# An FFT with a feed-forward layer on one core: fewer float32 units, an earlier split of w_out, one low half on VectorE, a longer hand-written order

## The chip, the cores and the metric

The kernel runs on one core of a Trainium2 chip. The metric is the device time of one execution in microseconds, lower is better. Engines are named as the profile does: PE (TensorE matmul), PEld (its weight loads), DVE (VectorE), ACT (ScalarE), POOL (GpSimd), SP (SyncE, whose queue issues most DMAs). L432 is line 432 of the kernel before.

## The reference

```python
# x: (8, 3008, 256) float32;  w_in: (256, 2048), w_out: (2048, 256), both float64
X = np.fft.fft(np.fft.fft(x, axis=1), axis=2).real.astype(np.float32)
X = X.reshape(8 * 3008, 256)
h = X @ w_in
g = np.where(h >= 1, h, np.where(h <= -1, 0.0, (h + 1) ** 2 / 4))
return (g @ w_out).astype(np.float32)
```

## The kernel before

**Mathematics.** The 3008 points of the sequence are taken as 47 x 64. Stage 1 multiplies by a 47-point transform (`stage1_sums`, the tiles `y` into a PSUM bank, copied to `z`), stage 2 by a 64-point one (`stage2_sums`, `z` into a bank, split into `pqh` and `pql` by `stage2_split`). The transform over the 256 channels is multiplied into w_in once, on the chip (`fold_w_in`, `fold_low`: the tiles `wh`, `wl`). Position s and its mirror image -s come out of the same two products: u - v and u + v.

**Number format.** float32 operands are split in a high part (`fp32r`, one pass of PE) and a low part, the remainder. A product is then three matmuls: high by high, low by high, high by low. "Native" units instead do one true float32 matmul in the second product, which the profile shows as two records. The weights come as float64 and are taken apart on the chip as integers: `convert_fields` (DVE), `convert_floats` (ACT, three instructions), `convert_join` and `convert_scale` (DVE), for 16 pieces of 128x512 (`jobs`): pieces 0, 1, 4, 5, 8, 9, 12, 13 are of w_in, the others of w_out. `split_w_out(q)` makes `woh` (ACT) and `wol` (DVE) from an eighth of w_out.

**Units.** A unit i is one batch b, one chunk k of columns (482, 512 or 512 wide) and one tile f of 128 of the 2048 inner features. There are 384. In batch 0, units 0 to 23 are features 0 to 7 for the three chunks, units 24 to 47 features 8 to 15. Each unit has
- `gemm1(i)`: 6 matmuls into two `uv` banks (of three in all); DVE makes `us` (L376) and the two halves of `h` (L378, L379); ACT makes `a` in two instructions (L382, L383);
- `activate(i)`: DVE takes min and max (L391 or L394). For units that aren't native, ACT copies the high part `gh` (L397) and POOL subtracts to get the low part `gl`, in two instructions of half a tile each (L399);
- `gemm2(i)`: the second product into four `acc` banks, issued in turn i + 4 (`LAG`).

**Order.** The main loop takes turns i = 0 to 387. A turn traces: `gemm1(i)`, then `activate(i - 1)` (or i, from `PINNED` on), then the letters of `STEPS[i]`, then pieces of the next batch's transform, then `gemm2(i - 4)`. Up to turn `PINNED` - 1 `pin()` chains each engine's instructions in just this order. Later instructions are placed by the compiler's scheduler, which may also put them into earlier gaps. The letters of `START` and `STEPS` are single steps: l load of a raw piece, x load of input, a b c v the four conversions, o `split_w_out`, f and s the two halves of the w_in fold, e `spread_delta` (PE writes a bank with tag `fft`, ACT copies it), p stage sums, z and w `stage1_copy` (w puts half on DVE), q `stage2_split`, y `fold_x`.

**Buffers.** Tiles of one tag share a few slots: `h` and `a` have three each, and the conversions of even pieces use `h`, those of odd pieces `a`. `fft` is one PSUM bank. The raw pieces of w_out and the later ones of w_in lie in the tiles `woh` and `wol` until the split needs these.

Of the kernel before, what the change touches and what calls it, by code (L numbers as in the profile page):

```python
# [37 lines left out]
def _constants():  # L38
# [26 lines left out]

START = (
# [3 lines left out]
)  # L70
STEPS = {
    0: "c4 v4 a5 b5",
    1: "c5 v5 a2 b2",
    2: "f2 f3 c2 v2 a3 b3 s2 s3",
    3: "e1 c3 v3 a6 b6",
    4: "c6 v6 p11 q11",
    5: "a7 b7",
    6: "c7 v7 p12 q12",
    7: "a8 b8",
    8: "c8 v8",  # L80
    9: "a9 b9",
    10: "c9 v9 a10 b10",
    11: "f4 f5 s4 s5",
    12: "e2 c10 v10 p13 q13",
    13: "a11 b11",
    14: "c11 v11 p14 q14",
    15: "o0 o1 a12 b12",
    16: "c12 v12 o2",
    17: "o3 a13 b13",
    18: "c13 v13 o4",  # L90
    19: "o5 a14 b14",
    20: "f6 f7 s6 s7",
    21: "e3 c14 v14 a15 b15",
    22: "o6 c15 v15",
    23: "o7",
}

RAW = {0: "gh", 1: "gh", 4: "gh", 5: "gh", 2: "woh", 3: "woh", 6: "woh", 7: "woh"}
RAW |= {8: "wol", 9: "wol", 10: "wol", 11: "wol", 12: "xt", 13: "xt", 14: "xt", 15: "xt"}

EARLY_BANKS = 13
NATIVE = NFT
PINNED = 18
NEXT = 18


# [1 line left out]
def fft_ffn_kernel(ctx: ExitStack, tc: tile.TileContext, x, cst, w_in, w_out, out):  # L108
    nc = tc.nc

    wts = ctx.enter_context(tc.tile_pool(name="wts", bufs=1))
    sb = ctx.enter_context(tc.tile_pool(name="sb", bufs=1))
    dr = ctx.enter_context(tc.tile_pool(name="dr", bufs=1, space=bass.MemoryType.DRAM))
    ps = ctx.enter_context(tc.tile_pool(name="ps", bufs=1, space=bass.MemoryType.PSUM))

    xt, yt, zt, nyb, pq = {}, {}, {}, {}, {}

    def load_x(b, q):
        tag = "xt" if b or q < 4 else "gl"
# [31 lines left out]
    def fft_bank(b, name):  # L151

        if b == 0 and early[0] < EARLY_BANKS:
            early[0] += 1
            return ps.tile([P, CH], F32, tag=f"acc{early[0] % 4}", name=name, bufs=1)
        return ps.tile([P, CH], F32, tag="fft", name=name, bufs=1)
# [6 lines left out]
    jobs = []  # L163
    for f4 in range(4):
        jobs += [("in", f4, 0), ("in", f4, 1), ("out", 2 * f4), ("out", 2 * f4 + 1)]
    raws, f32s, wo32, shared = {}, {}, {}, {}

    def load_w(n):
        kind, *at = jobs[n]
        if RAW[n] in ("woh", "wol"):  # L170
            if RAW[n] not in shared:
                shared[RAW[n]] = sb.tile([P, 4, CH, 2], U32, tag=RAW[n], name=f"raw_{RAW[n]}", bufs=1), iter(range(4))
            t, slots = shared[RAW[n]]
            raw = t[:, next(slots)]
        else:
            raw = sb.tile([P, CH, 2], U32, tag=RAW[n], name=f"raw_{n}", bufs=4)
        if kind == "in":
            src = w_in.bitcast(U32).rearrange("(h p) (o x) -> h p o x", p=P, x=2 * CH)[at[1], :, at[0] : at[0] + 1]
        else:
            m = CH // D * P  # L180
            src = w_out[at[0] * m : (at[0] + 1) * m, :].bitcast(U32).rearrange("(f p) x -> p f x", p=P)
        nc.sync.dma_start(raw.rearrange("p e two -> p (e two)").rearrange("p (f x) -> p f x", f=src.shape[1]), src)
        raws[n] = raw
# [24 lines left out]
    def convert_scale(n, eng):  # L208
        t, _ = cv.pop(n)
        kind, q, *_ = jobs[n]  # L210
        man, exp = (t[:, i].bitcast(F32) for i in range(2))
        dst = man
        if kind == "in":
            f32s[n] = man
        else:
            if q % 2 == 0 and q < 6:
                pair = sb.tile([P, 2, CH], F32, tag="gl", name=f"wo_{q // 2}", bufs=4)
                wo32[q], wo32[q + 1] = pair[:, 0], pair[:, 1]
            elif q >= 6:
                wo32[q] = man  # L220
            dst = wo32[q]
        eng.tensor_tensor(dst, man, exp, op=ALU.mult)
# [42 lines left out]
    s1, s2 = {}, {}  # L265
# [14 lines left out]
    def stage1_last(b, bank):  # L280
        pd = bank[:NA, GPC * 96 : GPC * 96 + 2 * NC]
        for m in range(2):
            nc.scalar.activation(zt[b][m * NA : (m + 1) * NA, :, P], pd[:, m * NC : (m + 1) * NC], AF.Copy)

    def stage1_copy(b, q, vector=False):
        z, bank = zt[b], s1.pop((b, q))
        if q == 0 and b:
            stage1_last(b, bank)
        pt = bank[:, : GPC * 96].rearrange("p (i n) -> p i n", i=GPC)
        for h in range(2):  # L290
            for m in range(2):
                src = pt[h * NA : (h + 1) * NA].rearrange("p i (t m c) -> p m c (i t)", t=2, m=2)[:, m]
                dst = z[m * NA : (m + 1) * NA, :, (2 * q + h) * 8 : (2 * q + h + 1) * 8]
                if vector and h:
                    nc.vector.tensor_copy(dst, src)
                else:
                    nc.scalar.activation(dst, src, AF.Copy)  # L297
    def stage1(b, q):
        for p in range(q, min(q + 2, XC)):
            if (b, p) in xt and (b, p) not in yt:  # L300
                fold_x(b, p)
        stage1_sums(b, q)
        stage1_copy(b, q)
# [55 lines left out]
    n_units = len(units)  # L359
    per = NCHUNK * NFT  # L360

    fronts, acts = {}, {}

    def gemm1(i):
        b, k, f = units[i]
# [20 lines left out]
    def activate(i):  # L386
        n = WIDTH[units[i][1]]
        h, a = fronts.pop(i)
        if i < NATIVE:
            g = sb.tile([P, 2, CH], F32, tag="gh", name=f"g_{i}", bufs=4)[:, :, :n]  # L390
            nc.vector.scalar_tensor_tensor(g, a, 1.0, h, op0=ALU.min, op1=ALU.max)  # L391
            acts[i] = (g,)
            return
        nc.vector.scalar_tensor_tensor(h, a, 1.0, h, op0=ALU.min, op1=ALU.max)  # L394
        gh = sb.tile([P, 2, CH], F32R, tag="gh", name=f"gh_{i}", bufs=4)[:, :, :n]
        gl = sb.tile([P, 2, CH], F32R, tag="gl", name=f"gl_{i}", bufs=4)[:, :, :n]
        nc.scalar.activation(gh, h, AF.Copy)  # L397
        for sg in range(2):
            nc.gpsimd.tensor_tensor(gl[:, sg], h[:, sg], gh[:, sg].bitcast(F32), op=ALU.subtract)  # L399
        acts[i] = gh, gl  # L400

    accs, parts, outs = {}, {}, {}

# [5 lines left out]
    def gemm2(i):  # L409
# [8 lines left out]
        for dh in range(2):  # L418
# [4 lines left out]
            for sg in range(2):  # L423
                acc = accs[dh * 2 + sg]
                if i < NATIVE:
                    wo_at = (f % 2) * D + dh * P
# [22 lines left out]
            elif last and i < n_units - 1:  # L449
                nc.sync.dma_start(out[b, k, dh].rearrange("s p t -> p s t")[:, :, :n], o[:, :, :n])  # L450

    warm = sb.tile([P, CH], F32, tag="us", name="warm", bufs=2)
    nc.gpsimd.memset(warm, 0.0)
    warm_bank = fft_bank(0, "warm")
    for _ in range(9):
        nc.tensor.matmul(warm_bank, warm[:, :P], warm, start=True, stop=True)

    n1 = XC

    def piece_sums(n):  # L460
# [25 lines left out]
        "s": fold_low,  # L486
        "o": split_w_out,
        "e": spread_delta,
        "t": lambda n: stage1_last(0, s1[0, 0]),
    }  # L490

    def run_steps(names):
        for s in names.split():
            steps[s[0]](int(s[1:] or 0))
# [16 lines left out]
    for i in range(n_units + LAG):  # L511
        if i < n_units:
            b, r = divmod(i, per)
            r0 = NEXT if b == 0 else 0
            if r == r0:
                pending = fft_pieces(b + 1) if b + 1 < NB else []
                done, total = 0, sum(w for w, _ in pending)
                if pending:
                    for q in range(4):
                        load_x(b + 1, q)  # L520
            gemm1(i)
            if b == 0 and r > per // 2 and r % (NFT // 2) == NFT // 2 - 2:
                load_parts(units[i][1])
            if i <= PINNED and i:
                activate(i - 1)
            if i >= PINNED:
                activate(i)
            run_steps(STEPS.get(i, ""))

            change = r % NFT == LAG  # L530
            while pending and (change or r % NFT != LAG - 1 and done < total * (r + 1 - r0) / (per - r0)):
                change = False
                w, f = pending.pop(0)
                f()
                done += w
                k1 = n1 + 7 - len(pending)
                if 4 <= k1 + 3 < XC:
                    load_x(b + 1, k1 + 3)
        if i >= LAG:
            gemm2(i - LAG)  # L540
        if i < PINNED:
            pin()
# [54 lines left out]
```

## Time and profile before

| | |
|---|---|
| median of 3 runs | 1781.17 us (1780.04 to 3464.34) |
| profiled execution, its own time | 1778.06 us |
| its span, first to last instruction | 1776.3 us |
| PE busy | 1744.0 us (98%), 7858 matmuls |
| DVE busy | 1438.4 us (81%) |
| ACT busy | 1344.3 us (76%) |
| POOL busy | 1164.7 us (66%) |

The page of the profile cuts the span into 40 slices of 44.4 us. The windows view sums each engine's busy time in any stretch that is asked for; the timeline view lists instructions in order of start, with the idle time before each in brackets and what ended it. A row of the timeline begins with start and duration in us. A busy PE is not PE at its peak: instructions overlap, and at half clock the same matmul counts double.

### The profile page before, as it was taken

The page shows a single profiled execution, that of the slowest core. Times are in us where ns is not written, and L with a number is a line of the kernel's source. Part 1 is how long each engine was busy: PE and PEld are TensorE (multiplying, and loading weights), DVE is VectorE, ACT ScalarE, POOL GpSimd, SP SyncE. Part 2 cuts the span into 40 slices and gives each one's busy share as a digit, 9 for nine tenths or more (in the row PEclk, how much of TensorE's full clock was granted, in tenths as well). Part 3 has the DMA queues.
Part 4 walks back from the last instruction along what each step waited for, and adds up shares of the span by engine and source line. Part 5 has one row for each costly group of instructions (what it writes and reads, how often), then busy time and mean ns, then how long its engine had stood idle before and what let it go on. Part 6 is the DMA issues. An engine that isn't in the chain of part 4 may idle for free.

```text
span 1776.3 us, 21601 instructions
## 1 busy us (share of the span) xinstructions
PE 1744.0 (98%) x7858; PEld 1407.5 (79%) x7858; DVE 1438.4 (81%) x1762; ACT 1344.3 (76%) x1575; POOL 1164.7 (66%) x813
## 2 busy tenths in 40 slices
PE   7989999999999999999999999999999999999998
PEld 5556788888888888888888888888888888887876
DVE  6979888788887788878878778877888788888886
ACT  5657876887777777778777877778778787777775
POOL 0005866876677766677667776677666766767776
PEclk8999999999999999999999999999999999999999
DMA  9003222110010110101001110011000000000000
GB/s 287 0 23 104 91 73 72 40 54 19 24 42 27 50 42 1 51 27 53 30 4 57 45 31 25 10 51 50 28 24 33 1 23 31 12 24 8 16 24 24
DMA packets 29962, 72.49 MB, mean 41 GB/s; under 512 B 2976, under 2 KB 8224, under 8 KB 29856
## 3 DMA queue, kind: packets, MB, share of 16 engines
q1 hardware_dynamic: 29820, 71.12, 12.3%
q8 instruction: 61, 1.00, 0.2%
q14 instruction: 45, 0.37, 0.1%
q10 hardware_dynamic: 36, 0.01, 0.0%
HBM read 43.31 MB, written 27.81 MB: 40 GB/s over the span
## 4 chain that ended last, share of the span: by engine, by line
PE 67%; POOL 9%; ACT 8%; DVE 8%; issue 6%; DMA 1%; POOLq 0%; ACTq 0%; SPq 0%; DVEq 0%
PE acc L432 42%; PE uv L373 21%; POOL gl L399 9%; DVE h L394 4%; ACT a L383 3%; ACT gh L397 3%; PE s L336 2%; ACT a L382 2%; PE s L274 2%; DVE h L378 1%; DMA x<-in_x_dram 1%; DVE h L379 1%; POOL y L129 1%; ACT z L297 0%; DVE us L376 0%
## 5 line engine op out<-in xcount | busy, mean ns | idle before, releaser
L399 POOL TENSOR_TENSOR gl<-h,gh 128x512 fp32r<-128x512 f32 (+1 forms) x736 | 1057.7, 1460 | 448.2 <-ACT gh L397 408.1
L394 DVE SCALAR_TENSOR_TENSOR h<-a,h 128x1024 f32<-128x1024 f32 (+1 forms) x368 | 555.0, 1508 | 220.3 <-ACT a L383 218.7
L397 ACT ACTIVATE gh<-h 128x1024 fp32r<-128x1024 f32 (+1 forms) x368 | 384.1, 1044 | 343.1 <-DVE h L394 330.5
L432 PE MATMUL acc<-gh,woh 128*128 128x512 f32 (+1 forms) x1472 | 585.9, 398 | 2.7 <-DVE o L443 1.6
L432 PE MATMUL acc<-gl,woh 128*128 128x512 f32 (+1 forms) x1472 | 574.5, 390 | 0.9 <-POOL gl L399 0.9
L432 PE MATMUL acc<-gh,wol 128*128 128x512 f32 (+1 forms) x1472 | 574.2, 390 | 0.0
L382 ACT ACTIVATE a<-h,biases 128x1024 f32<-128x1024 f32 (+1 forms) x384 | 431.7, 1124 | 38.4 <-DVE h L379 36.3
L383 ACT ACTIVATE a<-a 128x1024 f32<-128x1024 f32 (+1 forms) x384 | 398.9, 1039 | 7.5
L432 PEld LDWEIGHTS acc<-gh,woh 128*128 128x128 f32 x1472 | 277.3, 188 | 63.3 <-DVE o L443 4.8
L432 PEld LDWEIGHTS acc<-gl,woh 128*128 128x128 f32 x1472 | 277.2, 188 | 62.0 <-POOL gl L399 2.0
L373 PE MATMUL uv<-pqh,wh 128*128 128x512 f32 (+1 forms) x768 | 308.7, 402 | 12.5 <-DVE us L376 5.7
L432 PEld LDWEIGHTS acc<-gh,wol 128*128 128x128 f32 x1472 | 277.0, 188 | 54.4 <-issue 0.2
L378 DVE TENSOR_TENSOR h<-us,uv 128x512 f32<-128x512 f32 (+1 forms) x384 | 259.8, 676 | 66.3 <-POOL gl L399 22.5
L373 PE MATMUL uv<-pql,wh 128*128 128x512 f32 (+1 forms) x768 | 300.6, 391 | 0.0
L373 PE MATMUL uv<-pqh,wl 128*128 128x512 f32 (+1 forms) x768 | 300.4, 391 | 0.0
L376 DVE SCALAR_TENSOR_TENSOR us<-nyb,delta,uv 128x512 f32<-128x512 f32 (+1 forms) x384 | 278.9, 726 | 19.0 <-PE uv L373 18.7
L379 DVE TENSOR_TENSOR h<-us,uv 128x512 f32<-128x512 f32 (+1 forms) x384 | 256.3, 667 | 0.0
L373 PEld LDWEIGHTS uv<-pqh,wh 128*128 128x128 f32 x768 | 144.5, 188 | 57.9 <-DVE us L376 10.0
L373 PEld LDWEIGHTS uv<-pqh,wl 128*128 128x128 f32 x768 | 144.8, 189 | 32.0 <-issue 3.6
L373 PEld LDWEIGHTS uv<-pql,wh 128*128 128x128 f32 x768 | 144.7, 188 | 30.1 <-DVE pql L160 0.4
L129 POOL TENSOR_TENSOR y<-x 96x512 f32<-96x512 f32 x56 | 101.8, 1817 | 45.4 <-PE uv L373 37.9
L297 ACT ACTIVATE z<-s 64x192 f32<-64x192 f32 x246 | 83.4, 339 | 7.0 <-PE s L274 2.6
(61 smaller groups left out, 660.9 us busy)
## 6 DMA issues: line engine op xcount, KB each, us to landing
x<-in_x_dram SPq DMA_DIRECT2D x64, 384.0 KB, 3.3
out_dram<-o SPq DMA_DIRECT2D x26, 512.0 KB, 2.8
out_dram<-o SPq DMA_DIRECT2D x14, 482.0 KB, 2.9
nyb<-nyr SPq DMA_DIRECT2D x24, 256.0 KB, 3.2
raw<-in_moe_w_in_dram SPq DMA_DIRECT2D x6, 512.0 KB, 9.2
raw_woh<-in_moe_w_out_dram SPq DMA_DIRECT2D x4, 512.0 KB, 8.3
part<-o SPq DMA_DIRECT2D x4, 512.0 KB, 4.5
os<-part SPq DMA_DIRECT2D x4, 512.0 KB, 3.7
```

The lines of the kernel that those rows point to most:

```text
L129: (engine or nc.gpsimd).tensor_tensor(y, t[:, 0], t[:, 1], op=ALU.add)
L297: nc.scalar.activation(dst, src, AF.Copy)
L373: nc.tensor.matmul(t[:, :n], w[m][:, cols], r[:, m, :n], start=(j == 0), stop=(j == 2))
L376: nc.vector.scalar_tensor_tensor(us, nyb[b, k][:, :n], delta[:, f : f + 1], uv[0], op0=ALU.mult, op1=ALU.add)
L378: nc.vector.tensor_tensor(h[:, 0], us, uv[1], op=ALU.subtract)
L379: nc.vector.tensor_tensor(h[:, 1], us, uv[1], op=ALU.add)
L382: nc.scalar.activation(a, h, AF.Relu, bias=half, scale=0.5)
L383: nc.scalar.activation(a, a, AF.Square)
L394: nc.vector.scalar_tensor_tensor(h, a, 1.0, h, op0=ALU.min, op1=ALU.max)
L397: nc.scalar.activation(gh, h, AF.Copy)
L399: nc.gpsimd.tensor_tensor(gl[:, sg], h[:, sg], gh[:, sg].bitcast(F32), op=ALU.subtract)
L432: nc.tensor.matmul(acc[:, :n], w, g[:, sg], start=(begin and j == 0), stop=(last and j == len(terms) - 1))
```

## The change

- `NATIVE` goes from 16 to 8: units 8 to 15 do the second product in three fp32r matmuls.
- `woh` and `wol` are tiles of their own from the start. The raw pieces lie elsewhere (tags `xt`, `pqh`, `pql`). Pieces 10 to 15 are loaded in turns 7 and 11 instead of at the start. The splits o0 to o7 go from turns 15 to 23 to turns 4, 5, 7, 8, 14, 16, 24 and 26; the conversions of pieces 9 to 15 and the folds f4 to f7 move by one to three turns.
- Up to unit 27 the second half of `gl` is made by DVE, in a closure that turn i + 2 calls ahead of `gemm1(i + 2)`; POOL keeps the first half. From unit 28 on POOL makes both.
- `PINNED` goes from 18 to 28. In pinned turns `gemm2(i - 4)` is traced ahead of the next batch's pieces.
- In `START`, y7 goes ahead of w5, and two and four dummy matmuls of 128 columns (`keep_warm`, letter i) follow on p6 and p7. The dummies write the `fft` bank; `warm` goes to tag `a`.
- The copies of batch 0 into `z` no longer wait for each other.

```diff
-    "a0 b0 a1 b1 c0 v0 y0 p0 t0 z0 c1 y1 v1 p1 p8 z1 n0 l2 l3 l6 l7 n1 l8 l9 l10 l11 n2 l12 l13 l14 l15 "
-    "y2 y3 f0 p2 z2 p3 s0 y4 w3 f1 y5 p4 p5 y6 s1 w4 e0 p6 w5 y7 p7 w6 w7 p9 p10 q9 q10 a4 b4"
+    "a0 b0 a1 b1 c0 v0 y0 p0 t0 z0 c1 y1 v1 p1 p8 z1 n0 l2 l3 l6 l7 n1 l8 l9 n2 "
+    "y2 y3 f0 p2 z2 p3 s0 y4 w3 f1 y5 p4 p5 y6 s1 w4 e0 p6 y7 w5 i2 p7 w6 w7 i4 p9 p10 q9 q10 a4 b4"
 STEPS = {
     0: "c4 v4 a5 b5",
     1: "c5 v5 a2 b2",
     2: "f2 f3 c2 v2 a3 b3 s2 s3",
     3: "e1 c3 v3 a6 b6",
-    4: "c6 v6 p11 q11",
-    5: "a7 b7",
+    4: "c6 v6 o0 p11 q11",
+    5: "a7 b7 o1",
     6: "c7 v7 p12 q12",
-    7: "a8 b8",
-    8: "c8 v8",
-    9: "a9 b9",
-    10: "c9 v9 a10 b10",
-    11: "f4 f5 s4 s5",
-    12: "e2 c10 v10 p13 q13",
-    13: "a11 b11",
-    14: "c11 v11 p14 q14",
-    15: "o0 o1 a12 b12",
-    16: "c12 v12 o2",
-    17: "o3 a13 b13",
-    18: "c13 v13 o4",
-    19: "o5 a14 b14",
-    20: "f6 f7 s6 s7",
-    21: "e3 c14 v14 a15 b15",
-    22: "o6 c15 v15",
-    23: "o7",
+    7: "l10 l11 l12 l13 o2 a8 b8",
+    8: "c8 v8 o3",
+    10: "a9 b9",
+    11: "c9 v9 l14 l15",
+    12: "f4 f5 s4 s5",
+    13: "e2 a10 b10",
+    14: "c10 v10 o4 p13 q13",
+    15: "p14 q14 a11 b11",
+    16: "c11 v11 o5",
+    17: "a12 b12",
+    18: "c12 v12",
+    19: "a13 b13",
+    20: "c13 v13",
+    22: "f6 f7 s6 s7",
+    23: "e3 a14 b14",
+    24: "c14 v14 o6",
+    25: "a15 b15",
+    26: "c15 v15 o7",
 }
-RAW = {0: "gh", 1: "gh", 4: "gh", 5: "gh", 2: "woh", 3: "woh", 6: "woh", 7: "woh"}
-RAW |= {8: "wol", 9: "wol", 10: "wol", 11: "wol", 12: "xt", 13: "xt", 14: "xt", 15: "xt"}
-EARLY_BANKS = 13
-NATIVE = NFT
-PINNED = 18
+RAW = {0: "gh", 1: "gh", 4: "gh", 5: "gh", 2: "xt", 3: "xt", 6: "xt", 7: "xt"}
+RAW |= {8: "pqh", 9: "pql", 10: "xt", 11: "xt", 12: "xt", 13: "xt", 14: "pqh", 15: "pql"}
+EARLY_BANKS = 12
+NATIVE = NFT // 2
+PINNED = 28
...
-                    nc.scalar.activation(dst, src, AF.Copy)
+                    ins = nc.scalar.activation(dst, src, AF.Copy)
+                if b == 0:
+                    if q:
+                        tc.declare_no_dep(ins.ins, group="z", reason="other columns")
+                    tc.add_to_no_dep_group("z", ins.ins)
...
         nc.scalar.activation(gh, h, AF.Copy)
-        for sg in range(2):
-            nc.gpsimd.tensor_tensor(gl[:, sg], h[:, sg], gh[:, sg].bitcast(F32), op=ALU.subtract)
         acts[i] = gh, gl
+        low_half(i, h, 0, nc.gpsimd)
+        if i < PINNED:
+            lows[i] = lambda: low_half(i, h, 1, nc.vector)
+        else:
+            low_half(i, h, 1, nc.gpsimd)
+
+    def low_half(i, h, sg, eng):
+        gh, gl = acts[i]
+        eng.tensor_tensor(gl[:, sg], h[:, sg], gh[:, sg].bitcast(F32), op=ALU.subtract)
...
-    warm = sb.tile([P, CH], F32, tag="us", name="warm", bufs=2)
+    warm = sb.tile([P, CH], F32, tag="a", name="warm", bufs=3)
     nc.gpsimd.memset(warm, 0.0)
-    warm_bank = fft_bank(0, "warm")
-    for _ in range(9):
-        nc.tensor.matmul(warm_bank, warm[:, :P], warm, start=True, stop=True)
+    warm_bank = ps.tile([P, CH], F32, tag="fft", name="warm_bank", bufs=1)
+
+    def keep_warm(n, width=P):
+        for _ in range(n):
+            nc.tensor.matmul(warm_bank[:, :width], warm[:, :P], warm[:, :width], start=True, stop=True)
+
+    keep_warm(9, CH)
...
+            if i - 2 in lows:
+                lows.pop(i - 2)()
             gemm1(i)
...
-            if i <= PINNED and i:
+            if 0 < i <= PINNED:
                 activate(i - 1)
             if i >= PINNED:
                 activate(i)
             run_steps(STEPS.get(i, ""))
-
+        if i >= LAG and i < PINNED:
+            gemm2(i - LAG)
+        if i < n_units:
             change = r % NFT == LAG
...
-        if i >= LAG:
+        if i >= PINNED:
             gemm2(i - LAG)
```

More of the change, by code (lines that the diff above doesn't have):

```diff
@@ L165, in fft_ffn_kernel @@
         jobs += [("in", f4, 0), ("in", f4, 1), ("out", 2 * f4), ("out", 2 * f4 + 1)]
-    raws, f32s, wo32, shared = {}, {}, {}, {}
+    raws, f32s, wo32 = {}, {}, {}
     def load_w(n):
         kind, *at = jobs[n]
[L170 to L176, printed above, removed]
+        raw = sb.tile([P, CH, 2], U32, tag=RAW[n], name=f"raw_{n}", bufs=4)
         if kind == "in":
@@ L215, in convert_scale @@
         else:
-            if q % 2 == 0 and q < 6:
+            if q % 2 == 0 and q < NATIVE // 2:
                 pair = sb.tile([P, 2, CH], F32, tag="gl", name=f"wo_{q // 2}", bufs=4)
                 wo32[q], wo32[q + 1] = pair[:, 0], pair[:, 1]
-            elif q >= 6:
+            elif q >= NATIVE // 2:
                 wo32[q] = man
@@ L294, in stage1_copy @@
                 if vector and h:
-                    nc.vector.tensor_copy(dst, src)
+                    ins = nc.vector.tensor_copy(dst, src)
                 else:
-                    nc.scalar.activation(dst, src, AF.Copy)
+                    ins = nc.scalar.activation(dst, src, AF.Copy)
[3 more added lines that the diff above has]
+                    tc.add_to_no_dep_group("z", ins.ins)
     def stage1(b, q):
@@ L360, in fft_ffn_kernel @@
     per = NCHUNK * NFT
-    fronts, acts = {}, {}
+    fronts, acts, lows = {}, {}, {}
     def gemm1(i):
@@ L488, in fft_ffn_kernel @@
         "e": spread_delta,
+        "i": keep_warm,
         "t": lambda n: stage1_last(0, s1[0, 0]),
```

## Prediction

> **What bounds the kernel now.** I read the page, then the windows by stage, then the timelines of turns 0 to 28. u_i below is the start of `us` of unit i on VectorE: u_4 is 58.11, u_10 is 87.28, u_18 is 140.76 and u_28 is 201.81, and the first three windows are cut there.
>
> ```profile
> span 1776.3 us, 21601 instructions
> PE 1744.0 (98%) x7858; PEld 1407.5 (79%) x7858; DVE 1438.4 (81%) x1762; ACT 1344.3 (76%) x1575; POOL 1164.7 (66%) x813
> ```
>
> ```profile
> core 0: us, PE busy (x) PEld busy (x) DVE busy (x) ACT busy (x) POOL busy (x), PEclk, DMA share, GB/s
> 58.11:87.28 29.17, 29.17 (x95) 17.38 (x95) 26.96 (x42) 19.08 (x23) 0.00 (x0) 0.97 0.00 1
> 87.28:140.76 53.48, 48.72 (x149) 27.22 (x147) 41.28 (x62) 30.63 (x41) 1.88 (x3) 0.94 0.08 26
> 140.76:201.81 61.05, 54.76 (x241) 40.74 (x242) 55.29 (x66) 48.91 (x73) 43.29 (x32) 1.00 0.31 97
> 302.00:1702.00 1400.00, 1397.61 (x6448) 1156.56 (x6447) 1137.57 (x1357) 1085.06 (x1237) 997.73 (x689) 1.00 0.09 30
> ```
>
> From 302 to 1702 TensorE is busy 1397.61 of 1400 us, and the change leaves that code alone. So whatever the change wins or loses before u_28 reaches the end unshortened. Ahead of it TensorE sets the pace only in turns 4 to 9 (29.17 of 29.17); in 10 to 17 it misses 4.8 us, in 18 to 27 6.3 us, and VectorE is busy 26.96 of 29.17 and 55.29 of 61.05: there is hardly room on it for more.
>
> **Part 1, the head: a gain.**
>
> ```profile
> 24.49 0.69 DVE L129 TENSOR_TENSOR y<-x 96x512 f32<-96x512 f32 x1
> 25.32 1.64 PE L274 MATMUL s<-cs,y 96*128 96x96 f32 x8 [1.35 <-DVE y L129]
> 27.71 0.73 DVE L295 COPY z<-s 64x192 f32<-64x192 f32 x2 [1.89 <-ACT z L297]
> 26.00:28.00 2.00, 0.96 (x5) 0.72 (x4) 0.29 (x1) 0.67 (x2) 0.00 (x0) 0.50 1.04 400
> 28.59 3.75 PE L336 MATMUL s<-cs,z 128*128 128x128 f32 x16 [1.63 <-DVE z L295]
> 68.45 1.05 PE L336 MATMUL s<-cs,z 128*128 128x128 f32 x8
> ```
>
> p7 (25.32) waited 1.35 us for y7, which stood behind w5; ahead of it, y7 is done about 0.9 us earlier. The last `z` copies on VectorE (27.71) started when ScalarE's ended; without that tie they run beside them, 0.7 less. The clock was 0.50 and p9, p10 took 3.75 us for 16 records; at full clock 8 records take 1.05, so 2 x 0.9 when the dummies hold the clock (they lie in the waits and cost at most 0.4). p7 itself, 1.64, would be 0.9 like them, 0.7 less. Together 0.9 + 0.7 + 0.7 + 1.9 = **-4.2 us** for u_0; bounds 0 (clock still halved, raw loads in the way) and -4.6. Turns 0 to 3 keep their letters, and the loads that leave the head were waited for by nobody there: nothing.
>
> **Part 2, turns 4 to 9: the splits.**
>
> ```profile
> 63.67 0.71 DVE L376 SCALAR_TENSOR_TENSOR us<-nyb,delta,uv 128x482 f32<-128x482 f32 x1
> 67.03 0.42 DVE L193 TENSOR_SCALAR cv<-raw_woh 128x512 uint32<-128x512 uint32 x1
> 69.05 0.72 ACT L200 ACTIVATE cv<-cv,biases 128x512 uint32<-128x512 f32 x1
> 68.00 0.72 DVE L376 SCALAR_TENSOR_TENSOR us<-nyb,delta,uv 128x482 f32<-128x482 f32 x1 [0.55 <-PE uv L373]
> 73.56 0.71 DVE L376 SCALAR_TENSOR_TENSOR us<-nyb,delta,uv 128x482 f32<-128x482 f32 x1
> 78.03 0.75 DVE L376 SCALAR_TENSOR_TENSOR us<-nyb,delta,uv 128x512 f32<-128x512 f32 x1 [0.68 <-PE uv L373]
> 83.08 0.74 DVE L376 SCALAR_TENSOR_TENSOR us<-nyb,delta,uv 128x512 f32<-128x512 f32 x1
> 124.09 0.63 ACT L159 ACTIVATE woh<-wo 128x512 fp32r<-128x512 f32 x1 [0.36 <-DVE wo L222]
> 125.24 0.68 DVE L160 TENSOR_TENSOR wol<-wo,woh 128x512 fp32r<-128x512 f32 x1
> ```
>
> A split is a 0.63 us copy on ScalarE, then a 0.68 us subtraction on VectorE (0.6 from start to start). In turn 5 ("a7 b7 o1") ScalarE is in b7 until 69.77, 6.1 us after u_5; only then comes woh, ending at 6.7, and VectorE, whose next instruction is wol, stands from 3.8 on with us_6 queued behind it, and TensorE's `uv` banks behind that. u_6 falls 7.3 after u_5 instead of 4.33: +2.9. o0 (turn 4) and o3 (turn 8) follow VectorE work that outlasts the copy: +0.6 each. In turn 7 o2 precedes a8, and woh stands behind `a`: wol starts some 4.8 after `us`, and with 0.6 for it and 0.7 for a8 the turn takes 6.1 instead of 4.47 (73.56 to 78.03), +1.6. Turn 9 is the first of part 3: 6.0 instead of 4.2 (83.08 to 87.28), +1.8. Sum **+7.5**; bounds +2.4 (four subtractions alone) and +9.
>
> **Part 3, the low half on VectorE.** What the change buys is on TensorE:
>
> ```profile
> 114.67 3.43 PE acc L432 x8
> 241.54 2.80 PE acc L432 x12
> 113.27 1.40 PE uv L373 x6
> ```
>
> The chain has a native 512-wide second product at 3.43 us and three fp32r passes at 2.80: 8 x 0.63 = 5.0 us of TensorE, whose turn falls to 1.40 + 2.80 = 4.2. What it adds is a wait, and unit 17 of the kernel before shows every link of it:
>
> ```profile
> 137.58 0.74 DVE L376 SCALAR_TENSOR_TENSOR us<-nyb,delta,uv 128x512 f32<-128x512 f32 x1
> 139.03 0.68 DVE L379 TENSOR_TENSOR h<-us,uv 128x512 f32<-128x512 f32 x1
> 139.74 1.15 ACT L382 ACTIVATE a<-h,biases 128x1024 f32<-128x1024 f32 x1 [2.98 <-DVE h L379]
> 140.92 1.06 ACT L383 ACTIVATE a<-a 128x1024 f32<-128x1024 f32 x1
> 141.89 1.04 ACT L397 ACTIVATE gh<-h 128x1024 fp32r<-128x1024 f32 x1
> 143.00 3.14 POOL L399 TENSOR_TENSOR gl<-h,gh 128x512 fp32r<-128x512 f32 x2 [0.76 <-ACT gh L397]
> 143.48 1.54 DVE L160 TENSOR_TENSOR wol<-wo,woh 128x512 fp32r<-128x512 f32 x1
> 108.57 0.60 ACT L159 ACTIVATE pqh<-s 128x512 fp32r<-128x512 f32 x1 [0.77 <-PE s L336]
> 109.20 0.69 DVE L160 TENSOR_TENSOR pql<-s,pqh 128x512 fp32r<-128x512 f32 x1 [2.07 <-ACT pqh L159]
> ```
>
> In a pinned turn gh(i-1) stands on ScalarE behind both `a` instructions of unit i, which need h_i. It ends at 142.93, 5.35 us after u_17. The low half of unit i-1 needs it, and on VectorE it stands ahead of us_{i+1}. So u_{i+1} is at least 5.35 + 0.03 (VectorE's delay behind ScalarE, 109.17 to 109.20) + 0.60 (the subtraction) = **6.0 us** after u_i, however fast TensorE is; with 482 columns 5.8. Queued behind the waiting half are `us` and both `h` of the next unit, hence ScalarE's next `a` and TensorE's third `uv` bank. This holds from turn 9 to 27. Bounds for a turn: 4.2 (TensorE) and 6.0 + 1.25 (GpSimd first, below); I take 6.0, whose links are all rows.
>
> On top, in turns 10 to 27:
>
> ```profile
> 193.72 0.66 DVE L378 TENSOR_TENSOR h<-us,uv 128x482 f32<-128x482 f32 x1 [1.25 <-POOL gl L399]
> 158.53 1.27 POOL L129 TENSOR_TENSOR y<-x 96x512 f32<-96x512 f32 x1
> 106.45 2.08 PE L336 MATMUL s<-cs,z 128*128 128x128 f32 x8 [4.51 <-ACT delta L241]
> 39.68 0.77 PE L373 MATMUL uv<-pqh,wh 128*128 128x482 f32 x1 [2.31 <-DVE us L376]
> 40.00:42.00 2.00, 2.00 (x4) 1.01 (x4) 2.00 (x4) 1.70 (x2) 0.00 (x0) 0.50 0.99 367
> ```
>
> - Six pairs "copy on ScalarE, subtraction on VectorE" (o4, o5, o6, o7, q13, q14) stand behind gh and ahead of the low half: 6 x 1.2 = 7.2, and 2.2 where GpSimd or a11 falls between: 9.4.
> - Two folds (12, 22): two wh copies, a row and s4, s5 in that place: 2 x 2.9 = 5.8. They cost the same kind before, but beside native units.
> - Turn 11: c9, v9 and two evictions on VectorE, 1.3.
> - Turn 18: the first piece of batch 1 needs two folds of x on GpSimd (1.27 and 0.4) that now stand behind gl(17), 5.4 us into the turn; gemm1(19) is behind the piece on TensorE: +4.7, and 1.3 for a clock that such a wait halves (106.45: 2.08 after 4.51 idle): 6.0.
> - While a conversion or its result holds one of three `h` slots, h_i must wait for GpSimd's half of unit i-2, as at 193.72; 0.55 in eight turns: 4.4.
>
> Fourteen turns at 6.0 and the four of 482 columns at 5.8 make 107.2; with 26.9 on top 134.1, against 53.48 + 61.05 = 114.5 before: **+19.6**. In that the stall of 4.51 at 106.45 is gone already (e2 and p13 now lie in two turns). Bounds: -12 (rival A) to +28 (B).
>
> **The sum.** At u_28 TensorE leads by about one product, of which 2 us are won back: -2. -4.2 + 7.5 + 19.6 - 2 = +20.9 on the profiled execution's 1778.06 us (1.8 above its span): **1799 us**. The median shown, 1781.17, is 3 above that execution, so the forecast is 1.0% over the median. 2% of it, 35.6 us, is about what a measurement of this kernel tells from no change.
>
> **Rivals.**
>
> A, TensorE keeps the pace: 1762. If the low half finds gh ready, turns 4 to 9 stay at 29.2, turns 10 to 27 lose the 5.0 of native work, the stall of 4.51 and some 2.5 of half clock after it, and the head gains 4.2: -16. For it: 98% busy. Against it: row 141.89, which stands behind 140.92 in pinned order. This is the faster side.
>
> B, GpSimd gets there first: 1807. Both halves of gl start on the same gh. At 143.00 GpSimd began 0.07 us after it, and the subtraction at 143.48 lasted 1.54 instead of 0.68. If GpSimd wins in the ten short turns, each is 1.25 longer, less the 4.4 of slot waits: +8. Against it: VectorE reacts to ScalarE in 0.03 us.
> The Trainium skill ("SBUF — State Buffer", section "SBUF: two separate sides") says that the pair of ports is an exclusive lock, held by whichever starts first for its whole instruction. The trace agrees in kind (1.54); no run here shows a DVE and a GpSimd subtraction released at once.
>
> C, the clock falls in every long turn: 1819, slower by over 2%. A turn of 7.3 us or more leaves TensorE 2.5 to 3.4 idle; at 39.68 a wait of 2.31 was followed by clock 0.50. Eight such turns at 2.5 each, nothing hidden, are +20. It decides once gemm1 comes later than VectorE is ready for it. Against it: TensorE runs a product ahead, so most of that is hidden.
> The Trainium skill ("TensorE: Matmul & The Clock Gate", section "HAM oscillation — how this bites in real kernels") wants gaps above about 3.4 us for that. By it only turn 18 would cool and C would cost nothing; row 39.68 speaks against the rule, with one gap.
>
> D, the written order doesn't hold (the scheduler fills the gaps with later units): about 1782.
>
> **How the numbers follow.** Forecast (1788 to 1808) 0.55; A 0.2; B 0.12; C 0.07; D 0.06. The range reaches over B and most of the way to A and C: 1770 to 1815. Faster by over 2% (below 1745.5) 0.02, within 0.92, slower (above 1816.8) 0.06.
>
> **What would show it.** Right: `us` rows 6.0 apart in plain turns 10, 13, 17, 21; a low half on VectorE that starts 0.03 after gh with idle time before it put down to ACT gh; us_6 7.3 after us_5; p9 and p10 at 0.9 each with the first uv near 29; TensorE misses over 30 us between u_10 and u_28. Wrong: `us` rows 4.2 to 5 apart (A), GpSimd's gl ahead of VectorE's low half (B), clock near 0.5 through turns 11 to 18 (C).

## The result, and the profile after

The changed kernel takes 1805.76 us (median of 4 runs, 1803.62 to 1807.05) beside 1780.71 us for the kernel before on the same chip: a ratio of 1.0141, 95% interval [1.0121, 1.0161]. It is 1.4% slower, which is less than the 2% that count as a difference here and more than the measurement's uncertainty. One of the four runs of the kernel before took 3464.34 us and doesn't enter the ratio. The profiled execution took 1803.62 us, 25.6 more than that of before; the forecast was +20.9 and 1799.

In this and the next section a turn's length is the time from one `us` row to the next, and u_i is the start of `us` of unit i (DVE, line 375 of the changed kernel). The page's first lines after:

```profile
span 1801.8 us, 21728 instructions
PE 1751.7 (97%) x7902; PEld 1420.0 (79%) x7902; DVE 1448.0 (80%) x1782; ACT 1351.9 (75%) x1583; POOL 1159.5 (64%) x809
```

PE is busy 7.7 us more although, by the prediction's prices, it was given 5.0 us less to do; in turns 10 to 26 the granted clock, below, is lower than before (0.89 and 0.90 instead of 0.94 and 1.00), and the same matmuls then count longer.

Behind the written order one must count the `us` rows with care. DVE's timeline where it ends, in the changed kernel:

```profile
222.35 1.33 DVE L375 SCALAR_TENSOR_TENSOR us<-nyb,delta,uv 128x482 f32<-128x482 f32 x2
233.59 0.71 DVE L375 SCALAR_TENSOR_TENSOR us<-nyb,delta,uv 128x482 f32<-128x482 f32 x1
```

The first row holds two instructions: the scheduler starts `us` of unit 28 right behind that of unit 27, and 233.59 is u_29. From 222.35 to 233.59 there are thus two turns, 27 and 28. The stages are cut at u_27 for this reason, while the forecast's last stage began at u_28. The windows view of the changed kernel, cut at its own u_4, u_10, u_18 and u_27, then from u_27 and from u_33 to the end; the last two rows are those same tails in the kernel before:

```profile
core 0: us, PE busy (x) PEld busy (x) DVE busy (x) ACT busy (x) POOL busy (x), PEclk, DMA share, GB/s
55.97:92.64 36.67, 34.43 (x107) 19.31 (x106) 29.30 (x45) 22.41 (x28) 0.56 (x1) 0.97 0.21 71
92.64:152.09 59.45, 47.38 (x169) 32.03 (x169) 45.27 (x67) 36.01 (x45) 12.71 (x11) 0.89 0.10 30
152.09:222.35 70.26, 52.46 (x225) 40.36 (x226) 50.33 (x70) 45.65 (x68) 25.84 (x21) 0.90 0.17 55
222.35:1801.80 1579.45, 1571.66 (x7223) 1299.59 (x7222) 1283.52 (x1530) 1213.95 (x1381) 1116.86 (x769) 1.00 0.10 34
249.82:1801.80 1551.98, 1544.46 (x7109) 1276.32 (x7107) 1260.37 (x1502) 1193.31 (x1353) 1098.16 (x757) 1.00 0.10 32
```

```profile
195.93:1776.30 1580.37, 1572.39 (x7239) 1298.05 (x7237) 1279.38 (x1528) 1216.97 (x1387) 1121.69 (x773) 1.00 0.10 34
222.63:1776.30 1553.67, 1545.69 (x7106) 1274.93 (x7104) 1258.50 (x1502) 1193.88 (x1353) 1098.48 (x757) 1.00 0.10 32
```

The first number behind the bounds is the stage's length, the second PE's busy time in it. Beside the kernel before:

| stage | before | after | difference | forecast |
|---|---|---|---|---|
| start to u_0 | 34.35 | 30.86 | -3.5 | -4.2 |
| turns 0 to 3 | 23.76 | 25.11 | +1.35 | 0 |
| turns 4 to 9 | 29.17 | 36.67 | +7.5 | +7.5 |
| turns 10 to 17 | 53.48 | 59.45 | +6.0 | } +19.65 |
| turns 18 to 26 | 55.17 | 70.26 | +15.1 | } |
| behind u_27 | 1580.37 | 1579.45 | -0.9 | -2.1 |

The forecast of +19.6 was for turns 10 to 27; without turn 27 (5.8 by the forecast, 5.88 before) it is 128.3 - 108.65 = +19.65. Measured are +21.1. From u_10 to u_27 PE misses 12.07 + 17.80 = 29.9 us, against 4.8 + 6.3 before. The wait that was forecast is there, link by link. Timelines of DVE and ACT in turn 9 of the changed kernel:

```profile
86.65 0.74 DVE L375 SCALAR_TENSOR_TENSOR us<-nyb,delta,uv 128x512 f32<-128x512 f32 x1
88.82 1.15 ACT L381 ACTIVATE a<-h,biases 128x1024 f32<-128x1024 f32 x1 [2.89 <-DVE h L378]
90.00 1.06 ACT L382 ACTIVATE a<-a 128x1024 f32<-128x1024 f32 x1
90.96 1.04 ACT L396 ACTIVATE gh<-h 128x1024 fp32r<-128x1024 f32 x1
92.03 0.69 DVE L406 TENSOR_TENSOR gl<-h,gh 128x512 fp32r<-128x512 f32 x1 [2.12 <-ACT gh L396]
92.64 0.74 DVE L375 SCALAR_TENSOR_TENSOR us<-nyb,delta,uv 128x512 f32<-128x512 f32 x1
```

`gh` stands behind both `a`; DVE is idle 2.12 us for it, starts the low half 0.03 us after `gh` ends, and `us` can only follow that: 92.64 - 86.65 = 5.99. The forecast was 6.0. Turns 13, 17 and 23 take 6.01, 6.02 and 6.00. Turns 10 and 21, which the prediction named beside 13 and 17, take 6.39 and 6.42: there `h` waits for GpSimd's half as well, 0.50 and 0.53 us. The same view of turn 5, in which the split came behind the conversion:

```profile
67.51 0.72 ACT L195 ACTIVATE cv<-cv,biases 128x512 uint32<-128x512 f32 x1
68.14 0.61 ACT L160 ACTIVATE woh<-wo 128x512 fp32r<-128x512 f32 x1
68.79 0.69 DVE L161 TENSOR_TENSOR wol<-wo,woh 128x512 fp32r<-128x512 f32 x1 [2.87 <-ACT woh L160]
69.39 0.71 DVE L375 SCALAR_TENSOR_TENSOR us<-nyb,delta,uv 128x482 f32<-128x482 f32 x1
```

u_5 was at 62.13, so the turn takes 7.26 (forecast 7.3).

### The profile page after: what moved, and what is told of

Same layout as the page of the kernel before. It is cut to its first block, busy times and chain, and to the rows that moved or that the text cites. A ratio compares the mean times of both kernels' runs of the same rounds, so it can differ in the third digit from the quotient of the medians.

```text
span 1801.8 us, 21728 instructions
## 1 busy us (share of the span) xinstructions
PE 1751.7 (97%) x7902; PEld 1420.0 (79%) x7902; DVE 1448.0 (80%) x1782; ACT 1351.9 (75%) x1583; POOL 1159.5 (64%) x809
## 4 chain that ended last, share of the span: by engine, by line
PE 64%; POOL 8%; ACT 7%; issue 6%; DVE 4%; POOLq 0%; ACTq 0%; DVEq 0%
PE acc L438 40%; PE uv L372 20%; POOL gl L406 7%; DVE h L393 3%; ACT a L382 3%; ACT gh L396 2%; PE s L335 2%; ACT a L381 2%; PE s L269 2%; DVE h L377 0%; POOL y L130 0%; ACT z L292 0%; DVE h L378 0%; DVE o L449 0%; DVE gl L406 0%
## 5 line engine op out<-in xcount | busy, mean ns | idle before, releaser
L393 DVE SCALAR_TENSOR_TENSOR h<-a,h 128x1024 f32<-128x1024 f32 (+1 forms) x376 | 565.0, 1503 | 210.7 <-ACT a L382 209.1
L396 ACT ACTIVATE gh<-h 128x1024 fp32r<-128x1024 f32 (+1 forms) x376 | 392.3, 1043 | 336.1 <-DVE h L393 326.1
L438 PE MATMUL acc<-gh,woh 128*128 128x512 f32 (+1 forms) x1504 | 601.0, 400 | 4.5 <-ACT o L447 1.8
L438 PE MATMUL acc<-gl,woh 128*128 128x512 f32 (+1 forms) x1504 | 587.9, 391 | 0.9 <-POOL gl L406 0.9
L438 PE MATMUL acc<-gh,wol 128*128 128x512 f32 (+1 forms) x1504 | 588.0, 391 | 0.0
L438 PEld LDWEIGHTS acc<-gh,woh 128*128 128x128 f32 x1504 | 284.7, 189 | 67.5 <-DVE o L449 4.6
L438 PEld LDWEIGHTS acc<-gl,woh 128*128 128x128 f32 x1504 | 284.0, 189 | 63.8 <-POOL gl L406 2.0
L438 PEld LDWEIGHTS acc<-gh,wol 128*128 128x128 f32 x1504 | 284.0, 189 | 56.5 <-issue 0.8
```

Of the source, the lines that this page charges most:

```text
L438: nc.tensor.matmul(acc[:, :n], w, g[:, sg], start=(begin and j == 0), stop=(last and j == len(terms) - 1))
```

## The experiments

The theory: a DVE instruction that waits for ACT's latest instruction of the turn stands ahead of `us` in an in-order queue, and so a turn lasts as long as that chain; giving up native units exchanges 0.6 us of PE per unit, which was not short, for that chain. The rivals: TensorE or its clock sets the pace (A, C), GpSimd and the port do (B), or the written order is lost somewhere (D). "After" and "before" are the two kernels; each ratio is to before on the same chip, with its 95% interval.

### Both low halves on GpSimd

```diff
-        if i < PINNED:
+        if False:
             lows[i] = lambda: low_half(i, h, 1, nc.vector)
```

> The changed kernel with both low halves on GpSimd up to unit 27 as well; order, splits and head stay. Theory 1 (VectorE's half waits for ScalarE's gh and holds up the next us): the plain turns with three free h slots (9, 13, 16, 17, 23, 25) fall from 6.0 us to 5 or less. In the turns in which a conversion holds an h slot (10, 11, 14, 19 to 21) h must now wait for two GpSimd instructions behind gh, 1.28 + 3.2 + 2.6 = 7.1 us instead of 6.4. Net about -5 us on 1806. Rival (the pinned order as such, or VectorE's load, is the cost): no plain turn falls below 5.8, time within 2 us of 1806. Rival 2 (only the wait counts and slots do not): -20 us, to 1785.

1807.99 us, 1.0159 [1.0142, 1.0177], 2.2 us more than after where 5 less was expected. Some plain turns do get short (turn 9: 3.18, turn 17: 3.88, turn 25: 4.16), others that the expectation named don't (turn 16: 7.25, turn 23: 8.84). Where a conversion holds one of the three `h` slots, `h` waits for GpSimd's second half. DVE and POOL timeline of this kernel:

```profile
90.39 2.51 POOL L406 TENSOR_TENSOR gl<-h,gh 128x512 fp32r<-128x512 f32 x2 [40.95 <-ACT gh L396]
92.94 0.69 DVE L377 TENSOR_TENSOR h<-us,uv 128x512 f32<-128x512 f32 x1 [4.05 <-POOL gl L406]
100.04 0.69 DVE L377 TENSOR_TENSOR h<-us,uv 128x512 f32<-128x512 f32 x1 [3.36 <-POOL gl L406]
```

From 92.94 to 100.04 is 7.1 us a turn. u_9 to u_27 takes 138.7 against 135.7 after. So the half on DVE is no loss compared with the same half on GpSimd: both are late for the same `gh`, one holds the `us` queue, the other the slot.

### The low half behind `us` instead of ahead of it

The half of unit i - 2 is issued in `gemm1`, between `us` and the two `h` of unit i.

```diff
...
+        if i - 2 in lows:
+            lows.pop(i - 2)()
...
-            if i - 2 in lows:
-                lows.pop(i - 2)()
             gemm1(i)
```

> The changed kernel with VectorE's low half of unit i-2 traced between us and h of unit i instead of ahead of us: the same work, the same engines, one instruction moved past one other. Theory 1: us no longer waits for gh, so the chain of a turn loses us (0.66 to 0.85 us): plain turns with three h slots go from 6.0 to about 5.2, those where h waits for GpSimd's half stay at 6.4; six to eight turns gain, -5 us, about 1801. Rival (VectorE is simply full): every turn the same as before the move, 1806.

1801.21 us, 1.0121 [1.0104, 1.0138]: -4.6, near the -5 that was expected; the intervals of the two ratios overlap. u_9 to u_27 takes 132.7 instead of 135.7. The timeline of DVE:

```profile
87.81 0.74 DVE L375 SCALAR_TENSOR_TENSOR us<-nyb,delta,uv 128x512 f32<-128x512 f32 x1
90.01 0.69 DVE L408 TENSOR_TENSOR gl<-h,gh 128x512 fp32r<-128x512 f32 x1 [1.46 <-ACT gh L398]
91.86 0.69 DVE L379 TENSOR_TENSOR h<-us,uv 128x512 f32<-128x512 f32 x1 [1.16 <-POOL gl L408]
```

The same instruction on the same engine now waits 1.46 instead of 2.12 us, and holds `h` instead of `us`. Turns 9, 13, 17, 21 and 25 get shorter by 1.0 to 2.8 us (turn 9: 3.19 instead of 5.99). Turns 10, 11, 14, 18, 22 and 23 grow by 0.7 to 2.5, so 3.0 us are left. In the plain turns it is the place in the queue that costs, but the chain through `h` remains. How much of it reaches the end stays open: from u_33, with 7109 matmuls left in both, this kernel takes 1554.9 us and after 1552.0, so that in the two profiles the whole gain is given back, and the spans differ by what was won ahead of u_9.

### Sixteen native units, all else as after

```diff
-NATIVE = NFT // 2
+NATIVE = NFT
```

> The changed kernel with sixteen native units again; the low halves on VectorE are then left for units 16 to 27. Theory 1: turns 9 to 16 have no gh, so TensorE sets their pace again (4.8 us in a plain turn): from u_9 to u_18 about 52 us instead of 65.4, and 10 us less at the end, 1796. Rival (float32 matmuls cost TensorE 5.0 us more and it is the bound): 1806 to 1811.

1792.11 us, 1.0065 [1.005, 1.008]: 13.7 us less than after, with 5 us more work for PE in it. u_9 to u_18 is 52.1 instead of 65.4 (expected 52). Rival A falls: more work for TensorE and a shorter time. This one constant is over half of the loss.

### The head alone, on the kernel before

```diff
-    "y2 y3 f0 p2 z2 p3 s0 y4 w3 f1 y5 p4 p5 y6 s1 w4 e0 p6 w5 y7 p7 w6 w7 p9 p10 q9 q10 a4 b4"
+    "y2 y3 f0 p2 z2 p3 s0 y4 w3 f1 y5 p4 p5 y6 s1 w4 e0 p6 y7 w5 i2 p7 w6 w7 i4 p9 p10 q9 q10 a4 b4"
...
-EARLY_BANKS = 13
+EARLY_BANKS = 12
```

with the untied `z` copies and the `warm` tile and bank of the change.

> The kernel before with the head of the change alone: y7 ahead of w5, the six dummies, the warm tile and bank, and the z copies of batch 0 without ties. Theory: us of unit 0 starts near 30.9 instead of 34.35, and as TensorE is full behind it, most of the 3.5 us reaches the end: 1777 to 1779 against 1780.7. Rival: the turns 1 to 4 take it back (a clock that falls at another place, as in turn 2 of the changed kernel, 9.29 instead of 7.94): 1780 to 1781.

1776.98 us, 0.9983 [0.9973, 0.9992]: 2.9 us gained, u_0 at 30.57, and from there every turn up to 33 within 0.4 us of before. So a gain in the head does reach the end.

### The head without the dummies

After without `i2` and `i4`.

> The changed kernel without the six dummy matmuls by stage 2; y7 and the copies without ties stay. Theory (a wait of 2 us halves the clock): p9 and p10 take up to 3.7 us instead of 2.0, and u_0 comes 1 to 2 us later. Rival (by the rule of the Trainium skill, only gaps over about 3.4 us halve it; without dummies the gaps here are 1 to 1.5 us): p9 and p10 stay at 2.0 and u_0 comes no later, or 0.3 earlier for the dummies left out.

1805.55 us, 1.0137 [1.0119, 1.0156]; u_0 at 29.59. PE's timeline, first after, then without the dummies:

```profile
26.89 2.02 PE L335 MATMUL s<-cs,z 128*128 128x128 f32 x16
```

```profile
25.62 2.02 PE L335 MATMUL s<-cs,z 128*128 128x128 f32 x16 [0.92 <-DVE z L290]
```

p9 and p10 run at full clock with no dummy ahead of them: the gap that was left is 0.92 us, since y7 is early and the copies are untied. And in another execution of the same head (in the kernel with p13 moved, below) they ran slower, behind the dummies, with PE busy all the time and the clock at 0.50:

```profile
28.09 2.91 PE L340 MATMUL s<-cs,z 128*128 128x128 f32 x16
26.00:28.00 2.00, 2.00 (x11) 2.00 (x11) 0.72 (x2) 0.68 (x2) 0.00 (x0) 0.50 1.02 390
```

So in these profiles the dummies are neither needed nor enough. In the profiles of the twelve kernels with the whole new head u_0 lay between 29.8 and 35.2, and turn 2 took 7.9 to 9.3; 3.5 us read from one pair of profiles is within that.

### The first piece of batch 1 loaded and folded earlier

The four loads go to turn 16, the first fold of x to turn 17; nothing in the piece changes.

```diff
+            if i == NEXT - 2:
+                for q in range(4):
+                    load_x(1, q)
+            if i == NEXT - 1:
+                fold_x(1, 0)
```

> The changed kernel; the loads of batch 1's first inputs go from turn 18 to 16, and GpSimd's two folds for its first piece (y0, yd) from behind gl(17) in turn 18 to behind gl(16) in turn 17. Theory: the first piece no longer holds gemm1(19) up; turn 18 falls from 12.9 us to about 6.5, and 4 to 6 us less at the end, 1800 to 1802. Rival (the turn is long for its conversion or its clock, or TensorE makes the wait good later): turn 18 stays above 11, 1806.

1797.89 us, 1.0097 [1.0084, 1.0111]: -7.9, more than the -4 to -6 expected; 5.7 of them lie in turns 18 to 26 of the profile. GpSimd and TensorE in turn 18, after and then here:

```profile
157.97 1.71 POOL L406 TENSOR_TENSOR gl<-h,gh 128x512 fp32r<-128x512 f32 x1 [4.67 <-issue]
159.65 1.25 POOL L130 TENSOR_TENSOR y<-x 96x512 f32<-96x512 f32 x1
160.96 2.02 PE L269 MATMUL s<-cs,y 96*128 96x96 f32 x8 [10.32 <-POOL y L130]
```

```profile
152.86 1.26 POOL L130 TENSOR_TENSOR y<-x 96x512 f32<-96x512 f32 x1
154.17 2.02 PE L269 MATMUL s<-cs,y 96*128 96x96 f32 x8 [3.95 <-POOL y L130]
```

The fold no longer stands behind `gl`; turn 18 goes from 12.89 to 6.51, and TensorE's wait from 10.32 to 3.95.

### Order written out up to turn 31

The low halves stay as after (`if i < LOWS`, `LOWS = 28`).

```diff
-PINNED = 28
+PINNED = 32
+LOWS = 28
```

> The changed kernel with the written order kept to turn 31 instead of 27; low halves on VectorE still up to unit 27. Theory: turn 27's 11.2 us come from two of batch 1's pieces that the scheduler pulled ahead of the second product (TensorE waits 3.06 us for GpSimd's fold of y); in written order turn 27 takes about 6 us, but the pieces then come later, so the time stays within 3 us of 1806. Rival (that reordering is a loss of its own): 5 us less, 1801. Rival 2 (pinned turns are dearer than the scheduler's): 1808 or more.

1809.41 us, 1.016 [1.0144, 1.0176]: +3.6. The expectation of no more than 3 us either way was just missed. After, turn 27 is where the hand-written order ends. The scheduler puts two pieces of batch 1 ahead of the second product of unit 24, and starts `us` of unit 28 right behind that of unit 27. POOL, PE and the window of turns 27 and 28, after:

```profile
220.20 6.82 POOL L130 TENSOR_TENSOR y<-x 96x512 f32<-96x512 f32 x4
221.96 2.02 PE L269 MATMUL s<-cs,y 96*128 96x96 f32 x8 [3.06 <-POOL y L130]
222.35:233.59 11.24, 10.97 (x38) 9.28 (x38) 8.56 (x13) 7.25 (x13) 7.65 (x5) 0.57 0.71 204
```

TensorE waits 3.06 us for a fold and then works through 38 instructions at a clock of 0.57. The window of the same two turns in the longer order:

```profile
223.76:235.26 11.50, 8.81 (x30) 6.63 (x31) 8.36 (x13) 7.69 (x11) 2.23 (x2) 0.62 0.43 153
```

They take 5.74 + 5.76 = 11.50 us here and 11.24 after. So the place where the written order ends costs nothing, and the premise of the expectation, a single turn of 11.2 us, is wrong: it is two turns. From u_27 to u_33 after takes 27.5 us and this kernel 29.4 (before 26.7), with 7109 matmuls left in both. Rival D describes these turns, but there is no loss in them to explain, and a longer written order is slightly the worse one.

### The split ahead of the conversion in turn 5

```diff
-    5: "a7 b7 o1",
+    5: "o1 a7 b7",
```

> The changed kernel with o1 ahead of a7 and b7 in turn 5. Theory (wol waits on VectorE for woh, which stands behind b7 on ScalarE): woh then follows `a` at once, as o2 does in turn 7, and turn 5 falls from 7.26 to 6.05 us; all other turns stay. Rival (b7, or the load on VectorE, sets the turn): 7.2.

1800.94 us in one run. Turn 5 of this kernel:

```profile
65.62 0.61 ACT L160 ACTIVATE woh<-wo 128x512 fp32r<-128x512 f32 x1
66.26 0.69 DVE L161 TENSOR_TENSOR wol<-wo,woh 128x512 fp32r<-128x512 f32 x1 [1.66 <-ACT woh L160]
67.54 0.71 DVE L375 SCALAR_TENSOR_TENSOR us<-nyb,delta,uv 128x482 f32<-128x482 f32 x1
```

u_6 follows u_5 (61.50) by 6.04 (expected 6.05) instead of 7.26. One run can't say whether the end moves by 1.2; the turn does.

### Sixteen native units, and the first four splits back in turns 15 to 17

`native16` with o0 and o1 in turn 15, o2 in 16, o3 in 17.

> Sixteen native units as in native16, and o0 to o3 moved back from turns 4, 5, 7, 8 to 15, 15, 16, 17; the rest of the change stays. Theory (each early split delays us): turns 4 to 9 fall from 36.7 (33.9 in native16) to 28 to 30 us, and turns 15 to 17 grow by 2 to 3; against native16 (1792) -3 to -5, 1787 to 1789. Rival (TensorE, with 4.63 us a native turn, is the bound in turns 4 to 9 anyway, or the splits cost the same wherever they are): 1791 to 1793.

1792.63 us, 1.0067 [1.0053, 1.0081]: no difference from native16, where -3 to -5 was expected; the rival holds. Turns 4 to 9 fall from 33.9 to 29.6, but turns 15, 16 and 17 grow from 6.20, 6.51 and 6.00 to 7.44, 7.11 and 8.44, which is 4.3. In this order a split costs about as much in a later turn as in an early one, because there it stands in another chain of the same kind.

### p13 apart from the spread, on the kernel before with the new head

```diff
-    12: "e2 c10 v10 p13 q13",
-    13: "a11 b11",
+    12: "e2 c10 v10",
+    13: "p13 q13 a11 b11",
```

> The kernel before with the head of the change, and with p13 and q13 one turn later (13 instead of 12), away from e2, which leaves its result in the same PSUM bank. Theory: TensorE's stall of 4.51 us and the half clock behind it (2.5) go; turns 12 and 13, 12.1 and 4.8 us before, take 6 to 7 and 6; against head_alone (1777) another -4 to -6: 1771 to 1773. Rival (VectorE, which had 4 us of idle there, takes it back, or the wait moves to p14): 1776.

1773.59 us over five rounds, 0.9962 [0.995, 0.9975]: 0.4% faster than before, 3.4 us less than the head alone, where 4 to 6 less was expected; the intervals of the two ratios just overlap. TensorE:

```profile
101.71 1.05 PE L240 MATMUL delta<-biases,row 1*128 1x1 f32 x8
107.63 1.05 PE L340 MATMUL s<-cs,z 128*128 128x128 f32 x8
```

p13 takes 1.05 instead of 2.08 us and no longer waits 4.51 for the copy of the bank; turns 12 and 13 take 5.11 + 6.20 instead of 12.03 + 4.83. p13 takes 1.05 us in the change too, but there p14 behind it waits 3.26 us for `pql` and takes 2.08. Further on this profile doesn't show the gain: turns 17 to 20, in which the scheduler places units and pieces of batch 1, take 35.4 us instead of 29.6 (turns 19 and 20: 15.59 and 13.01), and from u_12 to u_28 it is 99.9 us as in the head alone (99.8), with 7109 matmuls left at u_33 against 7107. The profiled execution, 1777.2 us, was the slowest of the five. So where the 3.4 us of the medians lie stays open. This kernel and the next have the lowest medians of the study, below both before and after.

### The same with the early fold

> head_p13 with the loads of batch 1's first inputs in turn 16 and the folds y0 and yd in turn 17. In this kernel turn 18 is ordered by the scheduler, and TensorE waits 1.45 us there for the fold. Theory: turns 18 and 19 lose 3 to 8 of their 28.6 us, of which 1 to 4 reach the end: 1770 to 1773. Rival (the scheduler had covered the wait, and the loads wait for the raw pieces' slots): 1773 to 1775, as head_p13.

1773.55 us, 0.9965 [0.9952, 0.9979]: the same median. (The 28.6 us of the expectation are turns 19 and 20 by their units; here they take 26.1.) That fits the reading above: the early fold is worth 8 us where `gl` stands ahead of the fold, and in the order of before it doesn't.

### Three repairs of the changed kernel together

After with `NATIVE = NFT`, the early fold and o1 ahead of a7.

> The changed kernel with three of its costs taken away together: sixteen native units (native16), the early folds of batch 1 (fold_early), o1 ahead of a7 and b7 (o_first). It closes the account. Theory (the three lie in different turns, and TensorE is full from u_28 on, so they add): 1806 - 13.7 - 7.9 - 1.2 = 1783, within 2 us; turn 5 at 6.0, turn 18 at 6.5, u_9 to u_18 at 52. Rival (they share a cause, such as a clock that falls in long turns, or TensorE's lead swallows them): 1787 or more.

1784.22 us, 1.0023 [1.0013, 1.0032], inside the expected 1783 +- 2. Of the 25.1 us between the medians of after and before three edits take 21.5 back: 13.7 with the native units, and 7.9 more with the other two. Added up one by one they would be 22.8, so the costs add to within 1.3 us.

## Why the prediction was right

- **The mechanism.** `us` rows 6.0 apart, the low half 0.03 us behind `gh`, us_6 7.3 after us_5, and TensorE missing over 30 us between u_10 and u_28 were what the prediction asked for, and the trace has 5.99, 0.03, 7.26 and 29.9 (up to u_27). Restoring the native units takes 13.3 us out of turns 9 to 17, and moving the half takes 2.8 out of turn 9: the chain carries the loss in these turns. The time alone would not have told it: 1805.76 is nearer to rival B's 1807 than to 1799, and only the rows decide against B as the rule.
- **Turns 4 to 9: +7.5, as summed**: turn 4 +0.6, turn 5 +2.9, turn 7 +1.6, turn 8 +0.6, turn 9 +1.8.
- **Turns 10 to 17** come to some 59.4 if the terms are put into the turns that they name (the prediction gives no such split), and took 59.45.
- **Turns 18 to 26: +15.1 against some +13.7.** Turn 18 took 12.89 where its terms give 12.0, and the early fold, with which it takes 6.51, shows the cause. The terms of turns 24 and 26 were too small: these turns took 9.19 and 8.60 where the terms gave some 7.3 and 7.1. The other turns of the stage took 2.0 less than their terms together. In turns 24 and 26 GpSimd's half came ahead of a split and of DVE's half, rival B in place. Timeline of turn 24, all three engines:

```profile
203.43 1.04 ACT L396 ACTIVATE gh<-h 128x1024 fp32r<-128x1024 f32 x1
204.44 0.63 ACT L160 ACTIVATE woh<-cv 128x512 fp32r<-128x512 f32 x1
204.60 1.29 POOL L406 TENSOR_TENSOR gl<-h,gh 128x512 fp32r<-128x512 f32 x1 [4.51 <-issue]
205.11 1.33 DVE L161 TENSOR_TENSOR wol<-cv,woh 128x512 fp32r<-128x512 f32 x1 [0.70 <-ACT woh L160]
205.84 1.72 POOL L130 TENSOR_TENSOR y<-x 96x512 f32<-96x512 f32 x1
206.36 1.75 DVE L406 TENSOR_TENSOR gl<-h,gh 128x512 fp32r<-128x512 f32 x1
```

  A subtraction of 0.69 on DVE takes 1.33 beside GpSimd's half and 1.75 beside its fold, and each ends 0.55 us after the GpSimd instruction that started before it. This fits the exclusive port that the Trainium skill describes ("SBUF — State Buffer", section "SBUF: two separate sides"); what decides here is who stands ready first, and behind `woh` that is GpSimd. In plain turns DVE was first by its 0.03 us, so B failed as a rule for the whole.
- **Behind u_27: -0.9 against -2.1.** The prediction put 2 us of it on a lead of TensorE of about one product. At u_27 16 fewer matmuls are left than before (7223, 7239), at u_33 3 more (7109, 7106): the lead is there at u_27 and is used up within six turns. The tail from u_33 is 1.7 us shorter all the same; no run shows why.
- **The head: -3.5 against -4.2, and for a partly wrong reason.** The 1.9 us of p9 and p10 came (1.73), but because y7 and the untied copies closed the gap, not because of the dummies. By medians the head is worth 2.9.
- **Turn 2: +1.35 against 0.** The other turns of this stage are as before. In the profiles of kernels that are the same up to there turn 2 took 7.94 to 9.30, so one pair of profiles doesn't show it to be an effect of the change.
- **The rivals.** A fell with native16. C was wrong as a rule (clock 0.97, 0.89 and 0.90 in the three stages, and turns 13, 17 and 23 at 6.0), but the clock did fall in turns 27 and 28, and in turn 18, where TensorE waited 10.32 us:

```profile
154.00:156.00 2.00, 0.00 (x0) 0.00 (x0) 2.00 (x4) 1.31 (x2) 0.00 (x0) 0.50 0.00 0
```

  The Trainium skill ("TensorE: Matmul & The Clock Gate", section "HAM oscillation — how this bites in real kernels") asks for gaps above some 3.4 us. The waits of 10.32 and 3.95 and the gap of 0.92 agree with it; behind the 3.06 of turn 27, and with a clock of 0.50 from 224 to 226 us, eight records take 2.02 us, as they do behind the other two waits, which doesn't.

By stage the misses are +0.7 in the head, +1.35 in turn 2, +1.4 in turns 18 to 26 and +1.2 behind u_27, 4.6 us together and all to the same side, so no stage's miss was made good by another's. Inside the stages two things were lucky: in turns 18 to 26 +3.4 (turns 24 and 26) stands against -2.0, and the head's size came out in part for another reason than the one given.

## What to carry to other kernels

Before work is moved to an engine that is partly idle, read what the moved instruction waits for and what is queued behind it: an in-order queue turns a late operand into the period of the loop, and it makes no difference that the engine is only 80% busy. Work taken off an engine (here 5 us of TensorE) is worth nothing where that engine was waiting, and a shorter format that needs one more instruction on another engine's chain can cost more than it saves. And where a scheduler takes over, count the rows by their units: it may start one unit's instruction early, and what looks like one long turn is then two.

## What the runs showed of the hardware

The clock of the head isn't a property of the code: with the same instructions there p9 and p10 took 2.02 us in the kernel with the head alone and 2.91 in the one with p13 moved, in which the clock was granted at 0.50 while TensorE was busy 2.00 of 2.00 us. In that execution the dummies came too late: the clock fell between 22 and 24 us, the first of them started at 23.77. No wait of TensorE explains the fall. The last one before it, of 0.28 us, ended at 13.11, and from 14 us on every window of 2 us shows TensorE busy throughout:

```profile
22.00:24.00 2.00, 2.00 (x15) 1.99 (x15) 1.82 (x5) 0.73 (x3) 0.79 (x2) 0.82 0.74 280
```

Second, who gets the port. POOL's timeline in turn 9 of the changed kernel, beside DVE's 92.03 above:

```profile
92.08 1.77 POOL L406 TENSOR_TENSOR gl<-h,gh 128x512 fp32r<-128x512 f32 x1 [40.61 <-ACT gh L396]
```

Both halves were released by the same `gh`. DVE started 0.05 us earlier and its half lasted 0.69, as alone; GpSimd's lasted 1.77, against the 1.25 to 1.29 of the rows that started first. Where GpSimd was first, DVE's took up to 1.75.
